# Rebuilding the head of a fused attention and expert kernel: halved first loads, zero products in front, and batch 0's attention in one piece

## The chip, the cores and the metric

The kernel runs on one core of one Trainium2 chip. The metric is the device time of one execution in microseconds (us). The engines are named as in the profile: PE (TensorE matmul; PEld is its weight load), DVE (VectorE), ACT (ScalarE), POOL (GpSimd) and SP (SyncE, which here only issues loads and stores).

## The reference

A sliding-window attention over 8 batches of 8 heads, 576 positions, width 64, whose output is the input of a causal attention of four experts with a top-2 gate:

```
scores = (q @ k^T) / 8, kept where |i - j| <= 32
x = softmax(scores) @ v                     -> [8, 576, 512]
top 2 of x @ w_gate, softmax over the two   -> w
for e in 4 experts:  y_e = causal_attention(x wq[e], x wk[e], x wv[e]) @ wo[e]
out = sum over the chosen e of w_e * y_e
```

## The kernel before

One list, `ORDER` (L27), holds every step of all eight batches. A loop at the end of the kernel goes through it and calls the function that the step names, with the digits as arguments. No scheduler moves anything: each engine does its instructions in the order of the list, and semaphores hold an instruction until its inputs are there. After the `:` stands a letter: `a` ACT, `v` DVE, `g` POOL, and for loads `e` the SP queue, `f` the ACT queue. After the `@` stand the PSUM banks that the step uses.

A load or weight load (`load`, L183) also waits for the last matmul that stands before it in the list, so its place in the list is the earliest time of its issue. Loads ahead of the first matmul wait for nothing.

The steps of the windowed attention, with b the batch, g the group of four heads, h the half of the 576 queries, p the pair of heads:

- `lq b g part`, `lk b g part` load q and k of a group; part 0 is everything (576 KB), parts 1 and 2 are the first and the second nine of every 18 positions (288 KB each), so scores need both. `tq`, `tk` transpose them on DVE in two instructions (L293).
- `sc b g h @xy` makes the scores of a half in four banks: 80 PE instructions. `ex b g h p` exponentiates a pair on ACT (L338), `mk b g h p` multiplies it by the window's mask on POOL or DVE (L342).
- `lv b m` loads 128 positions of v (256 KB; m = 4 is the last 64). The windows of 64 positions begin at odd multiples of 32, so v is held twice, once moved by 64; `vc b par` makes the moved copy, all positions at once, for the lower or the upper 64 partitions.
- `av b T` is the product with v of the 128 queries from 32 + 128 T (T = 4: the first 32 and the last 32). T = 2 and 3 need only half 1, T = 0 and 1 only half 0. `un b T` divides by the sum on DVE, in two instructions (L369, L370).
- `xt b w` transposes the result back on PE (w = 1: queries of T = 2, 3; w = 0: T = 0, 1; w = 2: T = 4), `xf` copies it out of PSUM, `xb` casts it into XTB, the bf16 input of the experts.

Then come the experts: `lw n j` loads weights, `cw n j` casts them, `pp b j n` projects XTB to the experts' q or k (all of XTB of that half is needed), `pe` copies that out, `ps`, `xe`, `se`, `po` are the causal attention, `py` the output product.

Other steps of the head: `s_zero` clears a tile ZERO, `zz` does four matmuls of 512 columns on it whose result nobody reads, `s_ones` and `s_pads` write constants into the edges of tiles on DVE, `s_mask` and `s_ident` make the mask and the identity on POOL, `s_warm` a first exponential on ACT.

In the list of before, batch 0 is loaded as: q and k of group 0 whole, weights wk between them, group 1 in halves on two queues. `s_pads` stands behind the V copies. The scores of batch 1's group 0 (sc100, sc101) and their exponentials stand ahead of batch 0's av03. POOL's steps of the head, in order: mk0011, mk0010, mk0000, mk0111, mk0101, mk0110, s_ident, mk1010, mk1011, mk1001, vc10, xb00, cw00, mk1000, mk1101, mk1110, vc11.

## Time and profile before

| | us |
|---|---|
| runs of the kernel before, median of 3 | 236.63 (235.76 to 237.67) |
| span of the profiled execution, first to last instruction | 232.8 |
| PE busy in the span | 213.0 |
| DVE busy | 174.0 |
| ACT busy | 155.0 |
| POOL busy | 149.8 |

For the profiled execution the span is the time that is at hand; the runs' times are of other executions and hold some 4 us outside the span. The profile's times are counted from the span's start. A row of a timeline gives the start, the time until the last of the merged instructions has ended, the engine and line, the tiles, and in brackets how long the engine had been idle and what released it. The page's busy share of PE is high from its third slice on; the first 45 us are the part in which engines wait for one another.

### The profile page before, as it was taken

What the parts mean: (1) busy time and instruction counts of PE and PEld (TensorE: products, weight loads), DVE (VectorE), ACT (ScalarE), POOL (GpSimd) and SP (SyncE); (2) the same over time, 40 slices, a digit from 0 to 9 for tenths busy, and PEclk for the clock granted to TensorE, in tenths of its full rate; (3) what the DMA queues carried; (4) which work ended last, traced back from release to release, by engine and by line L of the source; (5) the groups of instructions that cost most, each with busy time, mean ns of one, the idle gap of its engine ahead of it and who ended that gap; (6) DMA issues with size and microseconds to landing.
All of it is one profiled execution on the core that took longest, in us unless ns stands there. A gap on an engine that the chain in (4) does not pass through costs nothing.

```text
span 232.8 us, 12298 instructions
## 1 busy us (share of the span) xinstructions
PE 213.0 (92%) x5516; PEld 170.0 (73%) x5516; DVE 174.0 (75%) x354; ACT 155.0 (67%) x237; POOL 149.8 (64%) x180
## 2 busy tenths in 40 slices
PE   3489799999999999999999999999999999899971
PEld 0356696887698778787898778988877877677530
DVE  2899968889879788675967987888678526773871
ACT  2146759857957778859657658586678697637841
POOL 6048778679736997699705799999646991510500
PEclk9999999999999999999999999999999999999999
DMA  7987889698775557755566684195446507035656
GB/s 207 401 299 163 186 222 214 167 272 227 257 203 161 167 147 221 199 157 158 168 160 206 169 213 139 28 249 192 105 92 167 149 6 234 4 90 172 222 190 231
DMA packets 60517, 41.96 MB, mean 180 GB/s; under 512 B 50736, under 2 KB 51760, under 8 KB 60464
## 3 DMA queue, kind: packets, MB, share of 16 engines
q1 hardware_dynamic: 60032, 40.32, 60.8%
q8 instruction: 43, 0.70, 1.3%
q10 hardware_dynamic: 432, 0.85, 1.0%
q14 instruction: 10, 0.08, 0.1%
HBM read 30.42 MB, written 9.44 MB: 171 GB/s over the span
## 4 chain that ended last, share of the span: by engine, by line
PE 57%; DVE 5%; DMA 5%; ACT 2%; issue 2%; DVEq 0%; SPq 0%; ACTq 0%
PE PS L178 53%; PE PS L181 5%; DMA out_dram<-Y 3%; DMA kn<-in_k_dram 2%; DVE XTF L172 1%; DVE Tkn L293 1%; DVE Y L172 1%; ACT XTB L170 0%; ACT VE L170 0%; ACT XTF L170 0%; DVE OE L571 0%; ACT A L338 0%; DVE GE L439 0%; DVE PS L569 0%; DVE m L441 0%
## 5 line engine op out<-in xcount | busy, mean ns | idle before, releaser
L342 POOL TENSOR_TENSOR A<-A,MASKP 128x576 f32<-128x576 f32 x60 | 84.2, 1423 | 17.0 <-ACT A L338 16.6
L515 ACT ACTIVATE ATE<-PS 128x1024 bf16<-128x1024 f32 x48 | 47.2, 1024 | 12.7 <-PE PS L178 12.0
L178 PE MATMUL PS<-Tqn,Tkn 32*64 32x128 f32 (+3 forms) x2560 | 46.1, 277 | 9.0 <-DVE Tkn L293 6.3
L338 ACT ACTIVATE A<-PS 128x576 f32<-128x576 f32 x64 | 38.5, 651 | 21.0 <-PE PS L178 20.9
L178 PEld LDWEIGHTS PS<-Tqn,Tkn 32*64 32x64 f32 x2560 | 40.3, 135 | 16.5 <-DVE Tkn L293 8.8
L518 POOL TENSOR_SCALAR_AFFINE_SELECT ATE<-ATE 128x256 bf16<-128x256 bf16 x64 | 24.6, 408 | 33.4 <-ACT ATE L515 33.4
L293 DVE STREAM_TRANSPOSE Tqn<-qn 128x576 f32<-128x576 f32 (+1 forms) x34 | 37.0, 1174 | 4.6 <-DMA qn<-in_q_dram 4.6
L293 DVE STREAM_TRANSPOSE Tkn<-kn 128x576 f32<-128x576 f32 (+1 forms) x34 | 37.4, 1179 | 3.9 <-DMA kn<-in_k_dram 3.9
L178 PE MATMUL PS<-V,A 128*64 128x65 f32 (+1 forms) x1280 | 38.8, 222 | 0.7 <-ACT V L170 0.5
L178 PEld LDWEIGHTS PS<-V,A 128*64 128x64 f32 (+1 forms) x1280 | 35.9, 132 | 3.8 <-issue 1.0
L172 POOL CAST XTB<-XTF 128x1024 bf16<-128x1024 f32 (+1 forms) x19 | 13.5, 724 | 17.5 <-ACT XTF L170 13.7
L370 DVE TENSOR_TENSOR XN<-PS,RC 128x512 f32<-128x512 f32 x32 | 22.1, 691 | 1.1
L170 ACT COPY Y<-PS 128x1024 f32<-128x1024 f32 (+2 forms) x19 | 15.3, 809 | 9.7 <-PE PS L178 6.1
L172 POOL COPY V<-V 64x2048 f32<-64x2048 f32 (+1 forms) x11 | 19.2, 1747 | 1.6 <-DMA V<-in_v_dram 1.2
L178 PE MATMUL PS<-WO,OTT 128*128 128x512 bf16 (+1 forms) x96 | 19.5, 346 | 0.5 <-ACT OTT L170 0.3
L178 PEld LDWEIGHTS <-ATE 128*128 128x128 bf16 x448 | 15.9, 97 | 4.0 <-issue 2.2
L178 PE MATMUL PS<-XTB,WQ 128*128 128x288 bf16 x128 | 18.3, 286 | 0.4 <-ACT A L338 0.4
L178 PE MATMUL PS<-WV,XTB 128*128 128x256 bf16 (+1 forms) x192 | 18.5, 256 | 0.0
L181 PE MATMUL PS<-ident,XN 128*128 128x128 f32 x144 | 18.5, 277 | 0.0
L178 PE MATMUL PS<-VE,ATE 128*128 128x65 bf16 x448 | 16.8, 193 | 1.7 <-ACT Y L170 0.9
L178 PE MATMUL PS<-XTB,WK 128*128 128x288 bf16 x128 | 18.1, 286 | 0.0
L178 PE MATMUL PS<-QKE 64*128 64x64 bf16 (+4 forms) x192 | 16.8, 277 | 0.6 <-ACT A L338 0.5
(77 smaller groups left out, 266.0 us busy)
## 6 DMA issues: line engine op xcount, KB each, us to landing
qn<-in_q_dram SPq DMA_DIRECT2D x15, 576.0 KB, 4.3
kn<-in_k_dram SPq DMA_DIRECT2D x15, 576.0 KB, 5.3
V<-in_v_dram SPq DMA_DIRECT2D x32, 256.0 KB, 4.0
out_dram<-Y SPq DMA_DIRECT2D x14, 512.0 KB, 3.6
V<-in_v_dram SPq DMA_DIRECT2D x8, 128.0 KB, 3.3
out_dram<-Y SPq DMA_DIRECT2D x16, 64.0 KB, 2.5
out_dram<-Y SPq DMA_DIRECT2D x3, 256.0 KB, 2.9
Y<-in_moe_wk_dram SPq DMA_DIRECT2D x2, 256.0 KB, 4.4
```

What stands on the lines that cost most here:

```text
L170: nc.scalar.copy(o, i)
L172: eng(c).tensor_copy(o, i)
L178: last_pe[0] = nc.tensor.matmul(*a, **kw)
L181: last_pe[0] = nc.tensor.transpose(*a)
L293: nc.vector.transpose(T[:, :].rearrange("q (p o) -> q o p", o=18)[:, o0:o1], n_[:, o0:o1, 32 * dh:32 * dh + 32])
L338: nc.scalar.activation(AT[(2 * b + g) % NAT_][half][p], two(b0)[:, :, 0:HS], EXP, scale=scale_att)
L342: eng(c).tensor_tensor(out=ap, in0=ap, in1=MASK[:, None, HS * half:HS * half + HS].to_broadcast([128, 2, HS]), op=MULT)
L370: nc.vector.tensor_tensor(out=XN[T // 2][:, T % 2, :].rearrange("p (g h d) -> p g h d", g=2, h=4), in0=u[:, :, :, 0:64], in1=rc[:, :, :, N ...
L515: nc.scalar.activation(chunk(ATE[(2 * b + j) % len(ATE)], ch), two(b0), EXP, scale=scale_moe)
L518: nc.gpsimd.affine_select(ap, ap, pattern=[[0, n], [1, w]], compare_op=IS_GE, fill=0.0, base=0, channel_multiplier=-1)
```

## The change

Only the start of `ORDER` is changed, up to sc110 (batch 1, group 1, half 1), and one function is new. From `sc110` on the list is the same.

- All q and k of batch 0 are loaded in eight halves on the SP queue, then k and q of batch 1's group 0, all ahead of the first matmul. The weights wk (`lw10`) come behind av03, and lq110, lk110 come behind sc010.
- `s_zero` and `s_pads` come first on DVE; all four `zz` come first on PE (sixteen matmuls).
- The scores of batch 0 are made in the order half 1, half 0 of group 0, half 1, half 0 of group 1.
- `vc00`, `vc01` are replaced by four `vd`, one for each 128 positions, in seven copies on ACT.
- av03, un03, av02, un02, av00, av01, av04 and xt01 of batch 0 follow at once on its masks. sc100 stands between av02 and av00, sc101 behind xt01. The masks mk0111 and mk0101 are on DVE (before: mk0001 and mk0100), and xf00 is on ACT (before: DVE).
- POOL's steps of the head are now: s_mask, s_ident, mk0010, mk0011, mk0000, mk0001, mk0110, mk0100, mk1010, mk1011, mk1001, vc10, xb00, cw00, and on as before.

```diff
-    lq000:e lw10 s_zero tq000:e lk000:e lq012:e lk012:e zz3@0 tk000:e lq011:f lk011:f s_ones tq012:e tk011:e lk100:e
-    tq011:e lq110:e lq100:e sc001@02 lk110:e lv02 s_mask cw10:a s_warm ex0010@0 sc000@46 tk012:e ex0000@4 zz2@0
-    ex0011@2 tq100:e sc010@04 mk0011:g tk100:e lv01 lv03 ex0100@0 ex0101@4 lv00 sc011@20 ex0001@6 mk0001:v tq110:e
-    mk0100:v tk110:e mk0010:g mk0000:g ex0110@2 sc100@46 lv04 ex0111@0 lv12 lw11 vc00:a ex1000@4 vc01:a s_pads
-    mk0111:g mk0101:g mk0110:g zz1@0 zz4@0 sc101@02 s_ident lv13 lw01 ex1011@2 lv11 av03@4 un03@4 ex1010@0 av02@2
-    un02@2 av00@0 lw00 av01@4 lq200:e un00@0 xt01@2 av04@0 un01@4 un04@0 xt00@4 ex1001@6 xf00:v@4 xt02@0 cw01:a
-    lk200:e xf01:a@2 sc110@62 xf02:a@0 lv22 lv10 mk1010:g tq200:e xb02:a lv23 tk200:e mk1011:g mk1001:g ex1101@2
-    sc111@04 xb01:a cw11:a vc10:g ex1110@0 xb00:g pp001@2 cw00:g mk1000:g mk1101:g mk1110:g vc11:g pp000@0 pe001:a@2
...
+    lq001:e lq002:e lk001:e lk002:e lq011:e lq012:e lk011:e lk012:e s_zero s_pads lk100:e lq100:e zz3@0 zz2@0 zz1@0
+    zz4@0 tq001:e tq002:e tk001:e tk002:e s_ones tq011:e s_mask s_ident s_warm sc001@02 lv03 lv04 lv02 tq012:e tk011:e
+    ex0010@0 sc000@46 lv01 lv00 ex0011@2 tk012:e mk0010:g ex0000@4 mk0011:g tq100:e sc011@02 ex0001@6 vd030:a mk0000:g
+    sc010@46 lq110:e ex0110@0 lk110:e ex0111@2 mk0001:g mk0111:v ex0100@4 mk0110:g tk100:e ex0101@6 vd020:a mk0100:g
+    mk0101:v av03@0 lw10 un03@0 av02@2 lv12 vd000:a tq110:e un02@2 sc100@46 lw11 ex1000@4 vd010:a av00@0 lv13 un00@0
+    av01@2 lw01 un01@2 ex1001@6 av04@4 un04@4 tk110:e lq200:e xt01@6 lv11 cw10:a xf01:a@6 sc101@02 ex1011@2 lw00
+    ex1010@0 xt00@4 xf00:a@4 xt02@0 lk200:e xf02:a@0 cw01:a sc110@62 lv22 lv10 mk1010:g tq200:e xb02:a lv23 tk200:e
+    mk1011:g mk1001:g ex1101@2 sc111@04 xb01:a cw11:a vc10:g ex1110@0 xb00:g pp001@2 cw00:g mk1000:g mk1101:g mk1110:g
...
+    def vd(c, b, m, par):
+        pairs = VSB[b % 2][:, :, :, 0:64].rearrange("p (m o) h d -> p m o h d", o=2)
+        if m < 3:
+            copy(c, pairs[0:64, m, 1], pairs[0:64, m + 1, 0])
+        copy(c, pairs[64:128, m, 1], pairs[64:128, m, 0])
```

## Rows read from the trace of the kernel before

**Rows 1.** Busy time by stretch: length, then each engine's busy us, PEclk, DMA share, GB/s
```profile
0.00:3.00 3.00, 1.74 (x4) 0.44 (x4) 0.27 (x1) 0.00 (x0) 2.26 (x7) 1.00 0.35 77
3.00:7.90 4.90, 0.15 (x1) 0.00 (x0) 2.92 (x3) 2.01 (x3) 1.61 (x6) 1.00 1.07 366
...
100.00:200.00 100.00, 99.35 (x2632) 82.19 (x2630) 74.32 (x155) 71.29 (x108) 73.66 (x85) 1.00 0.53 147
...
228.00:232.00 4.00, 0.00 (x0) 0.00 (x0) 0.69 (x1) 0.59 (x1) 0.00 (x0) 1.00 0.66 234
232.00:232.80 0.80, 0.00 (x0) 0.00 (x0) 0.00 (x0) 0.00 (x0) 0.00 (x0) 0.57 0.00 0
```

**Rows 2.** Timeline of PE, 0 to 45 us: start, us, engine, line, operation, tiles
```profile
1.26 1.89 PE L178 MATMUL PS<-ZERO 128*128 128x512 bf16 x4 [1.26 <-DVE ZERO L211]
...
9.71 3.95 PE L178 MATMUL PS<-Tqn,Tkn 32*64 32x64 f32 x144 [0.35 <-DVE Tkn L293]
13.59 1.05 PE L178 MATMUL PS<-ZERO 128*128 128x512 bf16 x4
...
29.88 1.09 PE L181 MATMUL PS<-ident,XN 128*128 128x128 f32 x8
...
32.78 2.51 PE L178 MATMUL PS<-Tqn,Tkn 32*64 32x96 f32 x160
35.22 1.29 PE L178 MATMUL PS<-XTB,WK 128*128 128x288 bf16 x8
36.93 1.14 PE L178 MATMUL PS<-XTB,WQ 128*128 128x288 bf16 x8 [0.42 <-ACT A L338]
...
43.15 2.03 PE L178 MATMUL PS<-V,A 128*64 128x65 f32 x62 [0.15 <-ACT A L338]
```

**Rows 3.** Timeline of DVE, 0 to 36 us
```profile
4.71 2.34 DVE L293 STREAM_TRANSPOSE Tqn<-qn 128x576 f32<-128x576 f32 x2 [3.51 <-DMA qn<-in_q_dram]
...
13.96 1.24 DVE L293 STREAM_TRANSPOSE Tkn<-kn 128x288 f32<-128x288 f32 x2
...
19.36 0.74 DVE L342 TENSOR_TENSOR A<-A,MASKP 128x576 f32<-128x576 f32 x1
...
22.18 1.36 DVE L342 TENSOR_TENSOR A<-A,MASKP 128x576 f32<-128x576 f32 x1
...
25.75 0.17 DVE L223 MEMSET XTF<- 128x128 f32 x1
...
27.87 0.14 DVE L369 RECIPROCAL RC<-PS 128x8 f32<-128x8 f32 x1
28.05 0.69 DVE L370 TENSOR_TENSOR XN<-PS,RC 128x512 f32<-128x512 f32 x1
```

**Rows 4.** Timeline of ACT, 0 to 38 us
```profile
23.77 1.90 ACT L170 COPY V<-V 64x2048 f32<-64x2048 f32 x1
25.68 1.74 ACT L338 ACTIVATE A<-PS 128x576 f32<-128x576 f32 x3
```

**Rows 5.** Timeline of POOL, 0 to 45 us
```profile
14.95 4.18 POOL L342 TENSOR_TENSOR A<-A,MASKP 128x576 f32<-128x576 f32 x3 [10.16 <-ACT A L338]
...
26.96 4.16 POOL L342 TENSOR_TENSOR A<-A,MASKP 128x576 f32<-128x576 f32 x3 [1.27 <-ACT A L338]
31.52 1.48 POOL L172 COPY V<-V 64x1536 f32<-64x1536 f32 x1 [0.40 <-DMA V<-in_v_dram]
33.96 1.04 POOL L172 CAST XTB<-XTF 128x1024 bf16<-128x1024 f32 x1 [0.96 <-DVE XTF L172]
...
40.52 2.42 POOL L172 COPY V<-V 64x2048 f32<-64x2048 f32 x1 [0.84 <-DMA V<-in_v_dram]
```

**Rows 6.** Loads issued at 0.81, 30.00 and 7.08: count, KB, us to landing
```profile
qn<-in_q_dram SPq DMA_DIRECT2D x1, 576.0 KB, 3.9
...
qn<-in_q_dram SPq DMA_DIRECT2D x1, 576.0 KB, 5.0
...
qn<-in_q_dram SPq DMA_DIRECT2D x1, 576.0 KB, 6.1
```

## The prediction

> **What bounds the kernel now.** I read the busy time by stretch first, then the timelines of PE, DVE, ACT and POOL over the first 45 us side by side, then the landings of the loads. From 100 to 200 us TensorE is busy for 99.35 of 100 us [rows 1], so behind the head the kernel runs at TensorE's pace: what the head loses or gains there is how late TensorE gets into that stretch, and nothing behind can win it back or lose it. The change ends at sc110; from there both lists are the same. So I follow two points that both kernels have: pp001, the first projection of batch 0 (starts at 35.22 before), and av12, the first attention output of batch 1 (starts at 43.15 before) [rows 2]. The forecast is the shift of av12.

> Why pp001 starts at 35.22 matters most. It reads XTB, and the last piece of XTB is xb00, a cast on POOL that runs from 33.96 to 35.00 [rows 5]. PE's own work before pp001 (sc110, sc111) runs from 32.78 to 35.29 [rows 2]. Both meet at 35. The head is therefore balanced between PE's list and POOL's list, and a change must move both. POOL's list ahead of xb00 is in both kernels: six masks of batch 0, then mk1010, mk1011, mk1001 (4.16 us together, from 26.96), then vc10 (1.48), then xb00 (1.04) [rows 5]. Engines work strictly in the order of the list, so xb00 can't start before mk1010, and mk1010 needs ex1010, which needs the scores sc101.

> **The change part by part.** *Loads.* The first q, 576 KB, lands 3.9 us after its issue at 0.81, at 4.7 [rows 6]. Now 288 KB come first. Bounds: 4.7 if the latency is fixed, and 0.8 less if the 288 KB that are gone count at the 366 GB/s of 3 to 7.9 us [rows 1]. I take 4.0, since bytes were moving for most of that time. The other halves follow at 0.8 us each, faster than DVE takes them (the 256 KB of wk ahead of the first k are gone too). Ten loads are now issued on SP without a wait; all of q, k of batch 0 should be in by about 9.6, and lk100, lq100 by 12.8 at that rate.

> *Transposes.* A half pair takes 1.24 us, a full pair 2.34, with the next one overlapping the end by some 0.15 [rows 3]: 1.1 and 2.2 in a row. From 4.0, four half pairs end at 8.4, s_ones 0.2, four more end at 13.0 (before, the last pair of batch 0 ends at 15.2 [rows 3]). *Pads*: 24 memsets, from 25.75 to un03's reciprocal at 27.87 [rows 3], now run between 1.2 and 3.4, while DVE waits for the first load. Price nothing; without that cover it would be 2.1. *Zero products*: sixteen at 1.89 us for four [rows 2] end by 1.26 + 7.6 = 8.8 at worst; the first scores need tk002's first half at about 8.0, so 0 to 0.8, and I take 0, since at the pace of the later four (1.05 us) [rows 2] they end sooner. The four of 13.59 and eight more vanish from the middle, where PE had to wait for DVE, or av03 for the V copies, in any case.

> *V copies.* Seven ACT copies of 64x512 take the place of one of 64x1536 and one of 64x2048. No row shows that size; a quarter of the 1.90 us [rows 4] is 0.48, a third more with a fixed part: 3.4 to 4.5 us in all, up to 1.1 more than before. ACT isn't what ends the waits below, so I cost it at nothing; vd030 waits for V's load, which comes behind the 12.8 of lq100, so about 14, where ex0110 behind it on ACT starts anyway.

> *Batch 0's attention at once.* Here the order costs. I go along the list, each step starting at the later of its engine and its inputs:
> - Scores sc001, sc000 end near 9.8 and 11.0 (1.25 us each at the pace of 160 in 2.51 [rows 2]); sc011 needs tk012 (13.0) and ends 14.1; sc010 15.3.
> - POOL starts masks at 10.6 instead of 14.95. Four, then mk0110 and mk0100, at 1.39 each [rows 5], end at 18.0 and 19.3. av03 needs mk0110: 18.0 to 19.05.
> - DVE: tq100 ends 15.2; mk0111 waits for ex0111 (15.4). A mask on DVE takes 0.74 in one row and 1.36 in the other, beside POOL's masks [rows 3]; POOL is at masks here, so 1.36: 16.8. tk100 19.0, mk0101 20.3, un03 (0.9, from 27.87 to 28.74 [rows 3]) 21.2.
> - tq110 now stands ahead of un02 on DVE. Its load lq110 isn't issued until sc010 is through (about 15.4; at 7.08 before). A lone load lands after 5.0 us, one behind others after 6.1 [rows 6]: 20.4 to 21.5. I take 20.4, hidden behind un03. tq110 ends 23.4, un02 24.3.
> - av01 writes the banks that un02 reads, so PE waits until 24.3: av01 25.3 (62 instructions in 2.03 us, so 1.05 for 32), av04 26.0 (as many, narrower ones; I take 0.7), xt01 27.1 (1.09), and only then sc101, 28.3 [rows 2]. ex1011 and ex1010 end 1.2 later, 29.5 (three in 1.74 [rows 4]).
> - POOL, idle since 19.3, starts mk1010 at 29.6: 4.16 + 1.48 + 1.04 put the end of xb00 at 36.3. Before: 35.0.

> So pp001 starts at 36.3, 1.1 us later than before, although PE reaches sc110 at about 29.8 (after ex1010's bank and xt02), 3 us earlier, and has finished sc111 at 32.3. PE's lead turns into a wait of some 4 us for POOL. From pp001 to av12 before passed 7.93 us, 0.57 of them two waits for ACT [rows 2]; that puts av12 between 43.7 and 44.2. By POOL: from xb00's end at 35.0 to vc11's end at 42.94 passed 7.94, of which 0.84 is a wait for V [rows 5] that the earlier loads may remove, 43.4. Before 43.15. I take +0.7. The profiled execution spans 232.8; the median of the runs is 236.63, 3.8 more, which lies outside the span. Forecast: 236.6 + 0.7 = 237.3.

> The unknown terms: with q001 as taken and both DVE masks at 0.74, pp001 comes at 35.1 and av12 at 42.3, -0.8. With the first load at 4.7 (+0.7), lq110 at 21.5 (+0.3) and vc10 stretched as vc11's 2.42 was [rows 5] (+0.9), av12 is up to 2.6 later. The likeliest case's own range is 235.8 to 239.2.

> **The rivals.** *PE keeps its lead.* If xb00 weren't awaited, that is if sc101 ended by 24.5 instead of 28.3 (the point from which it decides), the 3 us at sc110 would carry through: 233.6. For it: DVE starts and stays nearly without a gap, and the batch-0 masks start 4.3 us earlier. Against it: un02 stands behind 2.2 us of tq110, and sc101 behind av01, av04 and xt01; at its lowest prices the sum still gives 27. Chance 0.12.

> *The clock falls in the new wait.* [...] (The clock column reads 1.00 in 0 to 3 us too, where the products run at the lower pace, so it holds no record that early [rows 1].) At the end PE has nothing from 228 on; the column shows 1.00 up to 232 and 0.57 behind [rows 1]. So a wait of 4.0 us is close to what lost the level, and PE was then at scores of half pace for 4 us, up to the products of 13.59, before the level rose. Price: 4 to 5 us of work at half pace instead of full, +2.0 to 2.5, so 239.6. For it: the wait's length. Against: the level held for 4 us at the end. Chance 0.13.

> [...]

> *The loads don't come earlier, or lq110 comes late.* V's five loads and two q, k loads queue behind 3.4 MB; if lq110 lands at 22.5 or later, or the first halves don't land before 4.7 and lower the pace of the rest, everything from tq110 on moves by 1 to 2 us more: 239. Chance 0.07.

> **How the numbers follow.** The forecast 0.68, the lead kept 0.12, the clock 0.13, the loads 0.07. About 1% (2.4 us) is what a measurement of this kernel can tell from no change: below 234.3 is faster, above 239.0 slower. Faster: 0.12 and 0.01 from the forecast's edge, 0.13. Slower: 0.13 + 0.05 of the loads + 0.04 of the forecast's upper edge, 0.22. Same: 0.65. The range reaches from the forecast's lower end to the clock's price with its upper bound: 235.6 to 240.2, leaving out the lead kept and some 0.06 above.

> **What would show it.** Right: PE waits for POOL's XTB cast for about 4 us between 32 and 36.5, xb00 ends between 35.5 and 37, POOL waits about 10 us for ex1010 before a second run of masks at about 29.6, sc110 starts near 30, and DVE has no idle time between 4.2 and 15. Wrong: xb00 ends before 34, or pp001 follows sc111 without a wait; then some step between ex0111 and sc101 was over-priced, most likely tq110's place or the DVE masks. A granted clock under 1.00 behind the wait would show the clock rival; tq110 waiting for its load would show the loads.

## The result, and the profile after

The changed kernel takes 239.17 us (median of 20 runs, 235.83 to 241.36), the kernel before 236.63 (median of 20, 233.37 to 239.17). The ratio is 1.0108, 95% interval 1.0073 to 1.0142: slower by about 1.1%, some 2.5 us. The forecast was 237.3 with a range of 235.6 to 240.2 and "within 1%" as the likeliest outcome. The time is inside the range, the direction is the forecast's, the size is 1.9 us over it, and that puts the result just past the 1% bound: above 239.0 the prediction calls it slower, and it gave that 0.22. In the profiled executions the span grows from 232.8 to 235.3. A ratio here compares the runs within 1.5% of each kernel's fastest (by the medians of all runs e1 would be at 1.0072 instead of 1.0039, e9 at 1.0116 instead of 1.0046, and the others at most 0.4% elsewhere), and a profile is of one execution, a long one in e7 and e9 and a quick one in e6, e8 and the pair compared here, so a single row shows a place rather than a price.

The two points that the prediction follows come first. Timeline of PE in the changed kernel, 0 to 48 us (start, us, engine, line, operation, tiles, in brackets the idle time ahead and its releaser):

```profile
1.26 6.21 PE L178 MATMUL PS<-ZERO 128*128 128x512 bf16 x16 [1.26 <-DVE ZERO L211]
7.95 2.85 PE L178 MATMUL PS<-Tqn,Tkn 32*64 32x64 f32 x160 [0.48 <-DVE Tkn L293]
12.59 1.54 PE L178 MATMUL PS<-Tqn,Tkn 32*64 32x64 f32 x47 [1.79 <-DVE Tkn L293]
14.70 2.90 PE L178 MATMUL PS<-Tqn,Tkn 32*64 32x128 f32 x113 [0.57 <-issue]
17.53 0.68 PE L178 MATMUL PS<-V,A 128*64 128x65 f32 x14
19.18 0.80 PE L178 MATMUL PS<-V,A 128*64 128x65 f32 x20 [0.97 <-issue]
20.16 1.15 PE L178 MATMUL PS<-V,A 128*64 128x65 f32 x30 [0.17 <-ACT V L170]
21.23 1.37 PE L178 MATMUL PS<-Tqn,Tkn 32*64 32x96 f32 x78
24.93 0.32 PE L178 MATMUL PS<-Tqn,Tkn 32*64 32x64 f32 x2 [2.32 <-issue]
25.18 2.69 PE L178 MATMUL PS<-V,A 128*64 128x65 f32 x96
27.80 1.09 PE L181 MATMUL PS<-ident,XN 128*128 128x128 f32 x8
28.82 1.36 PE L178 MATMUL PS<-Tqn,Tkn 32*64 32x64 f32 x80
...
31.90 1.13 PE L178 MATMUL PS<-Tqn,Tkn 32*64 32x96 f32 x59
34.14 1.67 PE L178 MATMUL PS<-Tqn,Tkn 32*64 32x64 f32 x101 [1.10 <-issue]
38.69 1.14 PE L178 MATMUL PS<-XTB,WK 128*128 128x288 bf16 x8 [2.88 <-POOL XTB L172]
...
45.71 0.33 PE L178 MATMUL PS<-V,A 128*64 128x65 f32 x2 [0.15 <-ACT A L344]
```

pp001 (38.69) starts 3.47 us later than before and av12 (45.71) 2.56 later [rows 2]. From av12 to the end of the span passed 189.54 us, before 189.61: in this pair the whole difference lies in the head. The timeline of POOL shows who holds pp001:

```profile
10.45 5.53 POOL L348 TENSOR_TENSOR A<-A,MASKP 128x576 f32<-128x576 f32 x4 [4.80 <-ACT A L344]
...
31.55 4.13 POOL L348 TENSOR_TENSOR A<-A,MASKP 128x576 f32<-128x576 f32 x3 [11.38 <-ACT A L344]
36.18 1.47 POOL L172 COPY V<-V 64x1536 f32<-64x1536 f32 x1 [0.50 <-DMA V<-in_v_dram]
37.59 1.04 POOL L172 CAST XTB<-XTF 128x1024 bf16<-128x1024 f32 x1
```

POOL's first masks start 4.5 us earlier than before, the second run 4.6 us later, and xb00 ends at 38.63 instead of 35.00 [rows 5]. Between the two runs POOL has nothing to do for 11.38 us; before, the second run followed with a gap of 1.27.

A kind of wait that the prediction doesn't have has grown: "issue", time in which PE waited for nothing that the profile shows. From the waits of PE in 0 to 47 us (total, times, longest), in the kernel before:

```profile
PE PS L178 <- issue: 0.9, 1, 0.9
```

The same view of the changed kernel:

```profile
PE PS L178 <- issue: 5.0, 4, 2.3
```

And the clock: busy time by stretch of the changed kernel (length, the engines' busy us, PEclk, DMA share, GB/s), for the stretch in which the granted clock is lower: 0.50 of full from 13.35 to 16.76, called half level below. From 16.8 to 235.2 the column reads 1.00, full level:

```profile
13.30:16.80 3.50, 2.93 (x105) 2.53 (x94) 2.34 (x2) 1.27 (x3) 2.68 (x2) 0.51 1.06 168
```

### The profile page after: what moved, and what is told of

It reads as the page before. It is cut to its first block, busy times and chain, and to the rows that moved or that the text cites. A ratio compares the mean times of both kernels' runs of the same rounds, so it can differ in the third digit from the quotient of the medians.

```text
span 235.3 us, 12310 instructions
## 1 busy us (share of the span) xinstructions
PE 213.8 (91%) x5516; PEld 170.9 (73%) x5516; DVE 172.9 (73%) x357; ACT 156.8 (67%) x243; POOL 149.9 (64%) x180
## 4 chain that ended last, share of the span: by engine, by line
PE 72%; DMA 10%; DVE 5%; POOL 4%; issue 3%; ACT 3%; SPq 1%; DVEq 0%; ACTq 0%; POOLq 0%
PE PS L178 65%; PE PS L181 7%; DMA V<-in_v_dram 5%; DMA out_dram<-Y 3%; DMA kn<-in_k_dram 2%; POOL A L348 2%; POOL V L172 2%; DVE Tkn L293 1%; DVE XTF L172 1%; ACT A L344 1%; DVE Tqn L293 1%; SPq L184 1%; DVE Y L172 1%; ACT V L170 1%; ACT XTB L170 0%
## 5 line engine op out<-in xcount | busy, mean ns | idle before, releaser
L348 POOL TENSOR_TENSOR A<-A,MASKP 128x576 f32<-128x576 f32 x60 | 84.6, 1427 | 19.8 <-ACT A L344 19.3
L521 ACT ACTIVATE ATE<-PS 128x1024 bf16<-128x1024 f32 x48 | 47.2, 1024 | 14.0 <-PE PS L178 13.3
L178 PE MATMUL PS<-Tqn,Tkn 32*64 32x128 f32 (+3 forms) x2560 | 45.4, 273 | 7.1 <-issue 4.3
L344 ACT ACTIVATE A<-PS 128x576 f32<-128x576 f32 x64 | 38.5, 651 | 18.8 <-PE PS L178 18.4
L524 POOL TENSOR_SCALAR_AFFINE_SELECT ATE<-ATE 128x256 bf16<-128x256 bf16 x64 | 24.5, 406 | 34.2 <-ACT ATE L521 34.2
L178 PE MATMUL PS<-V,A 128*64 128x65 f32 (+1 forms) x1280 | 39.5, 222 | 2.1 <-issue 1.0
L178 PEld LDWEIGHTS PS<-V,A 128*64 128x64 f32 (+1 forms) x1280 | 36.4, 132 | 5.3 <-issue 2.0
L170 ACT COPY Y<-PS 128x1024 f32<-128x1024 f32 (+2 forms) x19 | 15.3, 810 | 10.6 <-PE PS L178 6.7
L178 PE MATMUL PS<-VE,ATE 128*128 128x65 bf16 x448 | 16.8, 193 | 1.9 <-ACT Y L170 1.1
L170 ACT CAST QKE<-PS 128x576 bf16<-128x576 f32 x19 | 12.0, 642 | 8.4 <-PE PS L178 8.3
```

Of the source, the lines that this page charges most:

```text
L170: nc.scalar.copy(o, i)
L178: last_pe[0] = nc.tensor.matmul(*a, **kw)
L344: nc.scalar.activation(AT[(2 * b + g) % NAT_][half][p], two(b0)[:, :, 0:HS], EXP, scale=scale_att)
L348: eng(c).tensor_tensor(out=ap, in0=ap, in1=MASK[:, None, HS * half:HS * half + HS].to_broadcast([128, 2, HS]), op=MULT)
L521: nc.scalar.activation(chunk(ATE[(2 * b + j) % len(ATE)], ch), two(b0), EXP, scale=scale_moe)
L524: nc.gpsimd.affine_select(ap, ap, pattern=[[0, n], [1, w]], compare_op=IS_GE, fill=0.0, base=0, channel_multiplier=-1)
```

## The experiments

Two theories went in. *A*: the order starves POOL (sc101 late, so ex1010, the second masks, vc10 and xb00 late), and PE's steps on the way there are late because its own instructions come in behind the loads. *B*: one misplaced wait (vd030 on ACT, un02 behind tq110 on DVE) does it, and moving it mends the kernel. The fall of the clock in the wait ahead of pp001, a rival of the prediction, was the third. Ratios are to the kernel before.

### e1: vd030 out of ACT's way

```diff
-    ex0001@6 vd030:a mk0000:g
+    ex0001@6 mk0000:g
...
-    ex0111@2 mk0001:g
+    ex0111@2 vd030:a mk0001:g
```

> The changed kernel with one step moved: the V copy vd030 stands behind ex0111 on ACT instead of ahead of ex0110. Theory A (the copy's 3.45 us wait for its V load holds ex0110 and ex0111, and with them mk0111 on DVE and all of DVE's list behind it): mk0111 starts near 15.8 instead of 17.44, un03 near 21.0 instead of 21.66, POOL's second run of masks 0.8 to 1.6 us earlier than 31.55, and the span is 0.8 to 1.6 us shorter than 235.3. Rival B (lq110's landing at 21.7 and PE's stalls without a releaser take over at once): mk0111 starts early all the same, but the second run of masks starts within 0.5 us of 31.55 and the span stays within 0.5 us.

Ratio 1.0039 (0.9995 to 1.0084). The 3.45 us that ACT waited for V ahead of ex0110 are gone, but mk0111 starts at 17.16 instead of 17.44: sc011 itself ends at about 15.8, since the clock was at half level from 13.67 to 20.49 here. The second masks start at 31.47, pp001 at 38.07, av12 at 46.50, because the clock was at half level again from 37.56 to 40.97 and pp001 to av12 took 8.43 us instead of 7.02. In this execution the wait that B names is worth 0.3 us of mask start; how it stands at full level, e2 shows (see the part on vd030 below). The ratio's interval reaches 1, so a part of the loss may be there; the trace doesn't show it.

### e2: un02 ahead of tq110

```diff
-    vd000:a tq110:e un02@2 sc100@46
+    vd000:a un02@2 tq110:e sc100@46
```

> The changed kernel with one step moved: un02 stands ahead of the two transposes tq110 on DVE. Theory A (av01 waits for banks that un02 frees, and un02 waits behind 2.2 us of transposes): un02 starts near 22.6 instead of 24.66, the scores sc101 start 1.0 to 2.0 us earlier than 28.82, POOL's second run of masks starts at 29.6 to 30.5 instead of 31.55, and the span is 1 to 2 us shorter. Rival B (PE itself, which stood for 2.32 us until 24.93 without a releaser inside sc100, sets this place): av01 and sc101 start within 0.6 us of where they did, and the span stays within 0.5 us.

Ratio 1.0077 (1.0035 to 1.0118). un02 starts at 21.89 instead of 24.66, and yet PE still waits from 22.99 to 24.52 for nothing shown, the second masks start at 31.15 and pp001 at 37.76. 2.8 us on DVE bring 0.4 at POOL's masks: DVE's place in the list wasn't the last thing that PE waited for.

### e3: xb00 off POOL's list

```diff
-    mk1010:g tq200:e
+    mk1010:g xb00:v tq200:e
...
-    cw11:a vc10:g ex1110@0 xb00:g pp001@2 cw00:g
+    cw11:a cw00:a vc10:g ex1110@0 pp001@2
```

> The changed kernel with two casts taken off POOL: xb00 on DVE ahead of tq200 (DVE stands idle there from 31.3 to 35.2), cw00 on ACT behind cw11. Theory A (POOL's list sets both pp001 and av12): the wait of 2.88 us for POOL is gone and pp001 starts near 36.5 instead of 38.69, held by xb01 on ACT; POOL's last V copy vc11 ends 1.65 us earlier, near 44.5, av12 starts near 44.5 instead of 46.2, and the span is 1.2 to 1.8 us shorter. Rival B (only pp001's place counts): the span is 2.2 us shorter. Rival C (neither; something behind 46 sets the end): within 0.5 us.

Ratio 1.0103 (1.0013 to 1.0194). Timeline of PE in e3, 30 to 48 us:

```profile
36.24 1.35 PE L178 MATMUL PS<-XTB,WK 128*128 128x288 bf16 x8
...
44.62 0.30 PE L178 MATMUL PS<-V,A 128*64 128x65 f32 x2 [0.20 <-issue]
45.59 2.61 PE L178 MATMUL PS<-V,A 128*64 128x65 f32 x82 [0.67 <-POOL V L172]
```

And of POOL:

```profile
32.50 4.62 POOL L348 TENSOR_TENSOR A<-A,MASKP 128x576 f32<-128x576 f32 x3 [12.51 <-ACT A L344]
...
43.23 2.31 POOL L172 COPY V<-V 64x2048 f32<-64x2048 f32 x1
```

Without xb00 on POOL, PE doesn't wait for XTB at all and pp001 comes 2.45 us earlier. av12 itself comes 1.1 earlier and then waits for vc11, the last step of the same POOL list; its second part starts at 45.59, against 46.24 in the changed kernel. POOL's late start holds the end of the head by two hands: take the first away, and the second is there 0.65 us sooner. The 0.65 is a lower bound: the clock was at half level from 25.81 to 29.22 here, and the second masks started 0.95 us later than in the changed kernel.

### e4 and e5: the scores of batch 1 that POOL waits for, first

e4 exchanges sc101, ex1011, ex1010 with sc100, ex1001, ex1000:

```diff
-    un02@2 sc100@46 lw11 ex1000@4
+    un02@2 sc101@46 lw11 ex1010@4
...
-    un01@2 ex1001@6 av04@4
+    un01@2 ex1011@6 av04@4
...
-    sc101@02 ex1011@2 lw00 ex1010@0
+    sc100@02 ex1001@2 lw00 ex1000@0
```

e5 puts both scores between batch 0's first products and moves V's loads, tq110 and vd030 to fit:

```diff
-    un03@0 av02@2 lv12 vd000:a tq110:e un02@2 sc100@46 lw11 ex1000@4
+    un03@0 sc101@46 lv12 ex1010@4 ex1011@6 av02@2 lv13 vd000:a un02@2 sc100@46 lv11 ex1001@6 ex1000@4 tq110:e
```

> The changed kernel with the two halves of batch 1, group 0 exchanged: sc101 (with ex1011, ex1010) where sc100 stood, ahead of av00, and sc100 (with ex1000, ex1001) behind xt01. So POOL's mk1010 and mk1011 can start 8 us earlier; only mk1001 waits as before. Theory A (POOL's 11.4 us wait for ex1010 alone is what makes xb00 late): the wait shrinks to about 3 us, a second one of about 5 us for ex1001 comes, the second run of masks ends near 32.5 instead of 35.7, xb00 ends near 35 and pp001 starts near 36.4, held by ACT: the span is 1.5 to 2.2 us shorter. Rival B (the V load lv11, which landed at 36.0, holds vc10 ahead of xb00 nearly as long): POOL waits for that load for about 3 us instead of 0.5, xb00 ends near 38.5 as before, and the span stays within 0.5 us.

> The changed kernel with batch 1's first scores moved up: sc101 stands behind av03 and sc100 behind av02 (banks 4 to 7, one after the other), their exponentials at once behind them, the V loads lv12, lv13, lv11 behind them in that order, tq110 behind un02, and vd030 behind ex0111. The front of the list is as in the changed kernel. Theory A (POOL starves because ex1010 comes late, and the V load lv11 came late too): POOL's idle time of 11.4 us shrinks to under 3, the second run of masks starts at 21 to 24 instead of 31.55, xb00 ends at 31 to 33 and pp001 starts at 32 to 34 without a wait for POOL; av12 starts 2 to 4 us earlier than in the changed kernel (45.7) and 1 to 2 us earlier than in the kernel before (43.15): ratio to the kernel before 0.990 to 0.997. Rival B (PE's stalls without a releaser and the half level of the clock make the loss): av12 no earlier than 45 and the ratio between 1.005 and 1.012.

e4: 1.0136 (1.0059 to 1.0214). POOL's masks of batch 1 start at 23.29 and 25.9, but vc10 then waits for V's load lv11 until 35.18, and xb00 runs from 36.60 to 37.64. e5: 1.0113 (1.0031 to 1.0194). Timeline of POOL in e5:

```profile
23.89 2.77 POOL L348 TENSOR_TENSOR A<-A,MASKP 128x576 f32<-128x576 f32 x2 [3.77 <-ACT A L344]
...
30.97 1.46 POOL L172 COPY V<-V 64x1536 f32<-64x1536 f32 x1 [1.96 <-DMA V<-in_v_dram]
34.61 1.04 POOL L172 CAST XTB<-XTF 128x1024 bf16<-128x1024 f32 x1 [2.19 <-ACT XTF L170]
```

The starvation is gone: 3.77 us instead of 11.38, the second masks 7.7 us earlier. xb00 still starts at 34.61, now behind xf00 on ACT; pp001 starts at 36.84 behind sc111, without a wait for POOL, and av12 at 45.97. POOL's wait was real, but right behind it stand V's load, then ACT's copy of the transposes, and PE's own list.

### e6: the two loads of batch 1's group 1 left out

```diff
-    sc010@46 lq110:e ex0110@0 lk110:e ex0111@2
+    sc010@46 ex0110@0 ex0111@2
```

lq110 and lk110 aren't loaded, so the scores of batch 1's group 1 are made from data of another group.

> The changed kernel without the two loads lq110 and lk110 (1.2 MB); batch 1's group 1 is computed from the data of batch 0's group 0 that still lie in the buffers, so its output is another one. The matmuls and their order are the same. Theory A (PE's stalls without a releaser are waits for its own instructions, which come by DMA in pieces of 16 KB and stand behind the loads' data): the stall of 2.32 us inside sc100 shrinks to under 1 us, av00 starts near 23.5 instead of 25.2, sc101 1 us earlier or more. Rival B (the stalls come from something else, so they don't care about the loads): the stall is still 1.8 us or more at the same instruction.

Timeline of PE, 20 to 50 us:

```profile
20.96 1.37 PE L178 MATMUL PS<-Tqn,Tkn 32*64 32x96 f32 x78
22.64 0.32 PE L178 MATMUL PS<-Tqn,Tkn 32*64 32x64 f32 x2 [0.30 <-issue]
...
25.09 1.75 PE L178 MATMUL PS<-V,A 128*64 128x65 f32 x64 [1.05 <-DVE XN L376]
...
37.11 1.95 PE L178 MATMUL PS<-XTB,WK 128*128 128x288 bf16 x8 [2.52 <-POOL XTB L172]
38.86 2.05 PE L178 MATMUL PS<-XTB,WQ 128*128 128x288 bf16 x8
40.74 1.14 PE L178 MATMUL PS<-XTB,WK 128*128 128x288 bf16 x8
```

The wait inside sc100, at the same two instructions, shrinks from 2.32 to 0.30 us: nothing but 1.2 MB of other data has gone. (At e9, which moves the two loads behind sc100, the wait there is gone as well.) The transposes behind it come 1.0 us earlier (26.77), since DVE's un02 then decides, and pp001 1.58. None of it arrives: the clock fell right behind the wait ahead of pp001 (half level from 37.28 to 40.70), eight products took 1.95 and 2.05 us instead of 1.14, and av12 starts at 45.81. The ratio is 1.0100 (1.0041 to 1.0159).

### e7, e11 and e12: products in the waits, to hold the clock

e7 puts four products on ZERO ahead of sc011 (zz5@0) and eight ahead of pp001, e11 only the eight, e12 the eight into the kernel of e6 (which leaves the same two loads out):

```diff
-    ex1110@0 xb00:g pp001@2
+    ex1110@0 xb00:g zz6@2 zz7@2 pp001@2
```

> The changed kernel with twelve more zero products: four ahead of sc011, where PE waited from 10.8 to 12.6, and eight ahead of pp001, where it waited for POOL. Theory A (the waits lose the clock's upper level, in the head at 13.4 to 16.8 in the changed kernel's profile and in the wait ahead of pp001 in three of the four others, and each loss in the second place costs 1.2 to 1.8 us): the clock reads 1.00 from about 7 us on to the end, from pp001 to av12 pass 7.0 to 7.5 us, and the ratio to the kernel before falls from 1.011 by 0.002 to 0.006. Rival B (the lower level is off the path): ratio within 0.002 of the changed kernel's. Either way the wait for POOL stays, and pp001 starts at 37.5 to 39.

> The changed kernel with eight more products on ZERO (512 columns each, four in 1.05 us, so 2.1 us) in the wait ahead of pp001, and nothing else. Clock theory: the level fell in the wait before pp001 in some executions and cost 1.4 to 1.7 us there; held by the products, no half level between 36 and 42 us, from pp001 to av12 7.0 us, and a ratio of about 1.006 to 1.008 (the profiled execution of the changed kernel, where the level did not fall there, is the lower end). Rival, that the ratio comes from the late first masks and POOL's list alone and the clock matters little: 1.010 as for the changed kernel. If the products push out pp001 (they end behind xb00), the ratio is above 1.011.

> As the run before, and without the loads lq110 and lk110 (batch 1's group 1 is computed from old data). Theory that the loads' crowding of PE's instructions and the clock's fall make up most of the loss: the wait inside sc100 is below 0.6 us, pp001 starts at about 37.1, av12 at about 44.1 instead of 45.71, no half level between 36 and 42 us: ratio 1.002 to 1.005. Rival, that something behind the head costs what the two runs share: 1.010 as without the products.

Ratios: e7 1.0202 (1.0111 to 1.0292), e11 1.0102 (1.0057 to 1.0148), e12 1.0141 (1.0092 to 1.0191). Timeline of PE in e11, 20 to 48 us:

```profile
25.44 0.32 PE L178 MATMUL PS<-Tqn,Tkn 32*64 32x64 f32 x2 [2.13 <-issue]
25.69 3.70 PE L178 MATMUL PS<-V,A 128*64 128x65 f32 x96
...
40.20 1.14 PE L178 MATMUL PS<-XTB,WK 128*128 128x288 bf16 x8 [1.50 <-POOL XTB L172]
```

The same of e12:

```profile
25.88 1.75 PE L178 MATMUL PS<-V,A 128*64 128x65 f32 x64 [1.47 <-DVE XN L376]
...
35.43 1.90 PE L178 MATMUL PS<-ZERO 128*128 128x512 bf16 x8
37.92 1.14 PE L178 MATMUL PS<-XTB,WK 128*128 128x288 bf16 x8 [0.59 <-POOL XTB L172]
...
44.95 0.33 PE L178 MATMUL PS<-V,A 128*64 128x65 f32 x2 [0.15 <-ACT A L344]
```

In all three the level is full from pp001 to av12, which takes 7.02 or 7.03 us. Elsewhere it fell: in e7 from 19.69 to 23.10 and again from 135.74 to 139.16; in e11 from 13.32 to 20.14 and then behind the wait in sc100 (half level from 26.97 to 30.38, the 96 products of 25.69 in 3.70 instead of 2.69). e12 has the shortest head of the three (no wait in sc100, level full from 20.27, av12 0.76 earlier than in the changed kernel), but 191.94 us behind av12 instead of 189.54, and its ratio is no better. So all three went against what was expected of them, e7 and e12 past their rivals too: the full level there didn't make the kernel shorter. The eight products don't push pp001 out: PE still waits 1.50 (e11) and 0.59 us (e12) for XTB behind them.

### e8 and e10: the front alone, in the kernel before

e8 takes from the change the loads in halves, k and q of batch 1 early, the pads first and lw10 late; e10 also all sixteen products in front. The order of batch 0's attention, the V copies and lq110, lk110 stay as before.

```diff
-    lq000:e lw10 s_zero tq000:e lk000:e lq012:e lk012:e
+    lq001:e lq002:e lk001:e lk002:e lq011:e lq012:e lk011:e lk012:e s_zero s_pads lk100:e lq100:e
...
-    tk000:e lq011:f lk011:f s_ones tq012:e tk011:e lk100:e tq011:e lq110:e lq100:e
+    tq001:e tq002:e tk001:e tk002:e s_ones tq011:e tq012:e tk011:e lq110:e
```

e10, against e8:

```diff
-    zz3@0 tq001:e
+    zz3@0 zz2@0 zz1@0 zz4@0 tq001:e
...
-    tk012:e ex0000@4 zz2@0 ex0011@2
+    tk012:e ex0000@4 ex0011@2
...
-    mk0110:g zz1@0 zz4@0 sc101@02
+    mk0110:g sc101@02
```

> The kernel before with one part of the change alone: q and k of batch 0 in eight halves on SP, then batch 1's first k and q, zero and pads first on DVE, and the weights wk behind lw11. The order of the scores, exponentials, masks, V copies and attention steps is that of the kernel before. Theory A (the front part is a gain and the rest of the change undoes it): tk012 ends near 13 instead of 15.2, the scores and POOL's masks move up by 1 to 2 us, pp001 starts at 33 to 34.5 instead of 35.22, and the ratio to the kernel before is 0.990 to 0.997. Rival B (V's loads, which now queue behind ten others, or the scores at the clock's lower level, take the gain back): ratio 0.998 to 1.004.

> The kernel before with two parts of the change: the loads in halves with zero and pads first, and all sixteen zero products in front; order of scores, masks, V copies and attention as before. Theory A (scores at the clock's upper level and no zero products in the middle are a further gain): POOL's masks start near 11 instead of 13.67 of the loads alone, PE's list is 1 to 2 us ahead of that kernel's at sc101, pp001 starts at 32.5 to 34.5, av12 at 40.5 to 42, ratio to the kernel before 0.988 to 0.997. Rival B (DVE's transposes and PE's waits for instructions set the middle anyway, faster scores only bring these waits forward, and the level falls in the gaps that the zero products filled): the clock shows 0.5 somewhere between 13 and 40, PE's waits without a releaser grow from 1.8 us to 3 or more, pp001 at 34.5 or later, ratio 0.999 to 1.008.

Ratios: e8 1.0010 (0.9960 to 1.0060), e10 1.0010 (0.9973 to 1.0047). Timeline of PE in e8:

```profile
34.68 1.29 PE L178 MATMUL PS<-XTB,WK 128*128 128x288 bf16 x8
...
42.49 3.73 PE L178 MATMUL PS<-V,A 128*64 128x65 f32 x120
```

The earlier loads and transposes are worth 0.66 us at av12 (42.49 against 43.15 [rows 2]). With the products in front as well (e10) pp001 is at 36.69 and av12 at 43.77: the clock rose early, fell at 13.32, behind a wait of PE of 1.79 us, and stayed at half level to 20.15. In the old order the front part of the change costs nothing that can be measured and brings nothing: both intervals end below the changed kernel's (1.0073 to 1.0142). The loss is in the rest: the new order, with its places of lq110 and lk110, and the V copies.

### e9: the order mended in five places

The changed kernel with un02, un00, un01 and un04 ahead of tq110, lq110 and lk110 behind sc100, vd030 behind ex0111, xb00 on DVE, cw00 on ACT and lv13, lv11 earlier (vd010 and some loads move along); two of the places:

```diff
-    sc010@46 lq110:e ex0110@0 lk110:e ex0111@2
+    sc010@46 ex0110@0 ex0111@2 vd030:a
...
-    tq110:e un02@2 sc100@46 lw11 ex1000@4 vd010:a av00@0 lv13
+    un02@2 vd010:a sc100@46 lw11 lq110:e lk110:e ex1000@4 av00@0 lv13 lv11
```

> The changed kernel with five places of the middle mended together: un03, un02, un00, un01, un04 ahead of tq110 and tk110 on DVE; the loads lq110 and lk110 behind sc100 instead of sc010, so that they are not on the way while PE fetches the instructions of sc100's end; vd030 behind ex0111 and vd010 ahead of ex1000 on ACT; xb00 on DVE and cw00 on ACT; the V loads lv13 and lv11 together behind av00. The front of the list is the changed kernel's. Theory A (the front is a gain, the order behind it and PE's waits for instructions take it away): the stall inside sc100 is under 1 us, sc101 starts near 26 instead of 28.8, POOL's second run of masks near 28, pp001 starts at 33 to 35, av12 at 41 to 43, ratio to the kernel before 0.990 to 0.998. Rival B (each mended wait is followed by another, the stall coming back one piece of instructions later, and tk110's late transposes holding sc110): pp001 at 36 or later, ratio 1.003 to 1.010.

Ratio 1.0046 (0.9995 to 1.0097), median 239.01. The waits that had been named are gone: sc100 runs without one, and pp001 starts at 36.03. But lk110 comes late, so tk110 is awaited (PE waits 2.34 us ahead of sc110), the clock was at half level from 31.30 to 34.72, av12 comes at 44.65, and 194.75 us follow it. What stands behind the head in that execution are PE's "issue" waits. From the waits of PE behind 47 us, in the kernel before:

```profile
PE PS L178 <- issue: 0.8, 2, 0.5
```

In e9:

```profile
PE PS L178 <- issue: 4.7, 7, 1.1
```

In e12, of the group above:

```profile
PE PS L178 <- issue: 2.2, 4, 0.8
```

No version beat the kernel before.

## Why the prediction was right, and where it was too low

**The mechanism held; its times came 2 us late.** PE's lead became a wait for POOL's cast of XTB, POOL waited for ex1010 between two runs of masks (11.38 us, forecast about 10), and av12 came later though the first scores came earlier. By the signs it had named, the kinds are right and the times are not: xb00 ended at 38.63 (35.5 to 37 was said), the second masks started at 31.55 (29.6), sc110 at 31.90 (30), and the wait for XTB was 2.88 instead of about 4. The front went as forecast: the first transposes start at 3.65 (4.0), tk002's end allows the first scores at 7.95 (8.0), and the last pair of batch 0 ends at 12.98 (13.0). Timeline of DVE:

```profile
3.65 2.34 DVE L293 STREAM_TRANSPOSE Tqn<-qn 128x288 f32<-128x288 f32 x4 [0.28 <-DMA qn<-in_q_dram]
...
17.44 1.45 DVE L348 TENSOR_TENSOR A<-A,MASKP 128x576 f32<-128x576 f32 x1 [1.74 <-ACT A L344]
...
21.00 0.73 DVE L348 TENSOR_TENSOR A<-A,MASKP 128x576 f32<-128x576 f32 x1
...
22.49 2.33 DVE L293 STREAM_TRANSPOSE Tqn<-qn 128x576 f32<-128x576 f32 x2
...
24.87 0.69 DVE L376 TENSOR_TENSOR XN<-PS,RC 128x512 f32<-128x512 f32 x1
```

The masks on DVE took 1.45 beside POOL's masks and 0.73 once POOL had ended (20.18): 1.36 was right for the first and too much for the second. lq110 landed at 21.73 (20.4), hidden all the same.

**The terms that were too small** add up to pp001 at 38.69 instead of 36.3:

- *sc011, forecast to end at 14.1, ended at about 16.0.* The step priced it at full level from 13.0 on. In the trace PE waits 0.57 us inside it, and the granted clock is at half level from 13.35 to 16.76. V's load was as late (see vd030). With ex0111 ending at 17.3 instead of 15.4, DVE's whole row moves: mk0111 ends at 18.9 (16.8), un02 at 25.56 (24.3). That is 1.3 of the 2.4 us.
- *sc100 and av00 aren't in the sum, so they were taken as hidden.* The wait of 2.32 us inside sc100 puts av01 behind PE instead of DVE; xt01 starts at 27.80 where 26.0 was forecast, 1.3 from DVE and 0.5 from here. e6 shows the cause of the wait: without two loads it is 0.30, and what is left is DVE's lateness.
- *V's load lv11* wasn't in the sum: it lands at 36.02, and vc10 waits 0.50 for it. e4 (vc10 at 35.18) and e5 (a wait of 1.96) show the same load in first place as soon as POOL's masks are early.

1.3 + 0.5 + 0.5 = 2.3 of 2.4. From pp001 to av12 passed 7.02 us, less than the 7.93 of before, mainly because the first eight products run in 1.14 instead of 1.29 and the wait of 0.42 for ACT behind them [rows 2] is gone; the sum had allowed for a part of that. So 1.5 to 2.0 too little at av12, and the forecast of +0.7 is a measured +2.56. That this is the upper end of the sum's own range (2.6) is luck: none of the three terms that made that end came about (the first load landed early, the wait for lq110 stayed hidden, vc10 took 1.47).

**vd030** was costed at nothing since V would land at "about 14". It landed at 15.45, and ACT waited 3.45 us:

```profile
15.47 0.62 ACT L170 COPY V<-V 64x512 f32<-64x512 f32 x1 [3.45 <-DMA V<-in_v_dram]
16.15 1.19 ACT L344 ACTIVATE A<-PS 128x576 f32<-128x576 f32 x2
```

The conclusion still held in this execution, for another reason: sc011 was as late as V. It isn't true in general. In e2, whose list is the same up to there, the level was full, sc011 ended at 14.67, and ex0110 still started only behind the copy. Timeline of ACT in e2:

```profile
14.91 0.62 ACT L170 COPY V<-V 64x512 f32<-64x512 f32 x1 [3.22 <-DMA V<-in_v_dram]
15.56 2.28 ACT L344 ACTIVATE A<-PS 128x576 f32<-128x576 f32 x4
```

There V's load alone costs about 0.9 us, and mk0111 ends at 18.31 (forecast 16.8). So V's load and PE's lateness were each enough, and the price of nothing for vd030 was wrong; the 0.3 us of e1 are its worth where PE is late as well.

**The clock rival** (0.13) came about, but not as an alternative: it comes on top, in some executions. In the changed kernel's profiled execution the level held through the wait of 2.88; in e1, e2, e4 and e6 it fell within or right behind that wait, and pp001 to av12 took 8.43 to 8.70 instead of 7.02. Its price is 1.4 to 1.7 us, less than the 2.0 to 2.5 forecast, which was 4 to 5 us at half pace: the stretch at half level there lasted 3.41 us in e1 and 3.42 in e6 (PEclk 0.83 from 37 to 47 us), and e6's first two rows of eight products took 1.95 and 2.05 us, 1.7 to 1.8 times the 1.14 of the next two. Length alone doesn't sort the waits: 4.0 us without a product kept the level at the end of the kernel before [rows 1], as did the changed kernel's 2.88, while e6's 2.52 and e4's 2.06 cost it. The clock of the 20 runs says more than the one profile: eight of them have a mean granted clock of 0.989 to 0.993, like the profiled one (0.993, one stretch of 3.41 us at half level), and their median is 238.28; twelve have 0.968 to 0.985, and their median is 239.97. So more time at half level goes with 1.7 us more, though where in the kernel it fell isn't shown, and the eight are still 1.65 us over the kernel before.

**Nothing behind the head could be won or lost** — that sentence was wrong as a rule. It holds for the pair of profiled executions (189.54 and 189.61). Over the runs of this study the time from av12 to the end lies between 188.6 (e6) and 194.8 (e9), with PE's "issue" waits there at 0.4 us in the one and 4.7 in the other. Over all fourteen profiled executions the two go together (correlation 0.92, some 1.6 us for each us of wait): 189.54 with 0.7 in the changed kernel, 191.94 with 2.2 in e12, 194.12 with 3.0 in e3. That is a correlation; no run changes these waits alone. The 3.8 us that the prediction put outside the span are two things as well: each run of the changed kernel reports 1.8 to 2.1 us more than its span, and the rest is that the profiled execution took less than the median (237.25 against 239.17).

**What stays open.** The order (with the V copies), not the front, costs the 1% (e8 and e10 at 1.001, the changed kernel at 1.011), and in the profiled pair all of it lies ahead of av12. The other profiles bear that out: av12 starts at 44.6 to 47.2 in the eleven with the new order and at 42.5 to 43.8 in the three with the old one. Behind av12 the old order has 189.6 to 189.7, the new one 188.6 to 194.8, so in most executions a second loss is added there. Which part of the order does it stays open: repairs at single places (e1 to e5) and e9's five together moved their own steps by 0.3 to 7.7 us and brought ratios of 1.004 to 1.014. The seven V copies by themselves, and xf00 on ACT, were not tried. e12 removed the wait in sc100 and the fall at pp001 and is at 1.014; in its profile what is left lies behind av12, where 2.2 us are "issue" waits. That its eight products move the places of these waits would fit, and isn't shown; one profiled execution a kernel doesn't tell it.

## What to carry to other kernels

When a stage is moved forward, look for the engine that is then starved and for what else its list holds: POOL's idle 11.4 us made the cast and the copy late that the next stage needs. Then look for what stands right behind it: with 7.6 of the 11.4 us gone (e5), a load and another engine's copy held the same cast. In a head where four engines and the loads are late within 2 us of one another, price a change as the shift of the last of them, and expect a repair at one to show the next. An estimate of PE's row in a stretch full of loads needs a term for the waits that show no releaser: 5.0 us in the first 47 of the changed kernel, 0.9 in those of before.

PE's "issue" waits go with DMA traffic: the one inside sc100 was 2.32 us with lq110 and lk110 loaded ahead of it and 0.30 without them (e6). Part 3 of the changed kernel's page (packets, MB, share of 16 engines) lists a queue of instructions:

```profile
q8 instruction: 43, 0.70, 1.2%
```

Each is one piece of 16,384 bytes. That they are PE's is an estimate from two counts: the page has 5,516 matmuls and as many weight loads, 11,032 instructions, which over 43 pieces is 256.6 each, and the waits are that far apart. The "issue" waits of the changed kernel that begin at 14.13, 18.21, 22.61 and 33.04 end 1.2 to 1.5 us behind the end of such a piece (13.25, 17.86, 23.43 and 32.97); so does the one of the kernel before (24.50, piece to 23.02). From wait to wait PE goes through the same number of instructions: 33 + 80 + 14 matmuls from the first to the second, 18 + 32 + 78 to the third (the 48th of sc011 on; a few records are missing), which with a weight load each is 254 and 256; the fourth comes after 255 more matmuls, 510 instructions, two pieces on. The piece for the end of sc100 started at 22.51 in the changed kernel, behind lq110 (landed at 21.73) and beside lk110 (issued at 18.11, landed 5.2 us later), at 22.97 in e11, and at 20.04 and 20.38 without these loads (e6, e12); the wait was 2.32 and 2.13, then 0.30 and none. Over the first 47 us the "issue" waits cost PE 5.0 us in the changed kernel, 2.5 and 1.8 without the two loads (e6, e12), and 0.9 in the kernel before.

The sixteen products in front raise the clock early (full level from 6.52) and don't keep it: it fell at 13.35, behind a wait of 1.79 us for DVE, when the scores of group 1 had begun. When it falls differs from one execution to the next: with the same products in front it held until 18.50 in e2, 19.74 in e5 and 25.81 in e3, but all twelve profiles with sixteen products in front lost it once in the first 26 us. In e8, with four products in front and twelve later, as before, it was full from 13.88 to 228.92. In e10, which differs from e8 in the place of those twelve, it was at half level from 13.32 to 20.15.
